# Order of the start of a fused forward and backward kernel: inverse phases earlier, filler transposes out, a small load moved ahead of a large one

## The chip, the cores and the metric

The kernel runs on one core of a Trainium2 chip, as one launch. The metric is device time in microseconds (us), the median of several runs. Engines are named as the profile names them: PE is TensorE's matmul, PEld its weight load, DVE is VectorE, ACT is ScalarE, POOL is GpSimd, SP is SyncE, which issues nearly all DMA transfers here (SPq and ACTq in the profile are the instructions that issue a transfer).

## What is computed

The reference is a forward pass and its whole gradient. With `xn = layernorm(q)`, S = 2048, D = 512, F = 1376, all in bf16, the output is `q + A + B`:

```
ks[t]  = sum over j of k[t-j] * shift_k[:, j]          (4 taps)
kv     = ks * v
y      = irfft(rfft(kv, 2S) * rfft(ssm_k, 2S))[:S] + kv * ssm_D
A      = xn * y
B      = ((xn @ w_gate) * (xn @ w_up)) @ w_down
out    = q + A + B;   then the vjp for grad_out with respect to
         q, k, v, shift_k, ssm_k, ssm_D, w_gate, w_up, w_down
```

So there are ten outputs. The long convolution is done by matrix products with tables of sines (a two stage transform), so the kernel has no FFT.

## The kernel before, in words

The sequence of 2048 rows is laid as 128 partitions times R = 16 rows; the feed-forward part B goes in NCH = 8 chunks of 256 rows, and within a chunk over NFB = 11 blocks of 128 columns of F, two blocks at a time (`ffn1`, L496 to L537). For each pair PE makes `pgu` (gate and up, 16 matmuls, L511) and `pdh` (gradient through w_down, 8 matmuls, L517); ACT copies them out of PSUM as `gu` and `dh` (L235, the helper `act`), and DVE multiplies them into `hd` (L532, L533). `yb` (L539 to L561) makes the products that need a whole chunk, `py` (11 matmuls) and `px` (22).

Beside this main work runs a side generator, `side`: `front()` (L712) and then `groups()` (L737). `front()` normalizes the rows of block b (`norm`, L316: statistics on DVE, a square root on ACT, the scaling of `x_b` on DVE), loads `kh` (all of k, shifted, in three transfers L312 to L314), transposes `ssm_k` (`kernel_spec`, L408: `ptk` on PE, `kn` on ACT) and puts the first transform of three signals through `stage1` (L361): `pf` on PE, copied out as `fst`, by ACT or, for the first signal's even rows, by DVE, and stored. `pre(b)` (L377) makes `dy_b` and `ks_b` (four taps, from `kh`) and `v_b` for that. The mixture of main and side is set by `pace` and `acc` (L770, L875 to L894): after each yield of the main work `acc` grows by `pace`, 170/71, and for each whole 1 the side is driven one step. `acc` starts at `-3 * pace[0]`. The result is a program order; from L657 to the call `first.close()` in `tables` DVE, ACT and PE keep it as written, and afterwards a scheduler may reorder, with `high_priority` (SOON) for evictions.

Transfers: SP issues them in one order, and they use eight semaphores in turn, so a transfer waits until the one eight places before it has landed. The weights come in three pieces, `WPARTS` (L642): blocks 0 and 1, 2 to 5, and 6 to 10. The first is issued from ACT. In the kernel before SP's list starts with x of block 0, grad_out of block 0, the second and third weight pieces with x of block 1 between them, grad_out of block 1, `ssk` (ssm_k, 2 MB, L649), then v 0, x 2, grad_out 2, v 1, and then `skr` (shift_k on one partition, 4 KB, L654) and `Drow` (ssm_D, in the tile `rows`, L655).

Tables: the class `Tables` (L34) makes the phases of the sine tables. The forward ones are made on DVE (`forward_base`, `forward_phases`). For the inverse ones `inverse_base` (L145) takes six small DVE instructions on a column and five on POOL, `inverse_phases` (L159) seven on POOL; its result `tii` is folded on DVE (`inverse_fold`, L174) and goes through the sine on ACT as `zi` (`inverse_sin`, L177). `tables(n)` (L678) places the rest of this behind the steps of chunk 0. `warm(src, n)` (L476) issues n transposes whose result nobody reads; it is called with 36 at the start, 10 after the normalization, and 40 behind the transposes of w_down's third piece (L530).

PSUM: `P2` has three buffers of two banks, used by `pgu`, `pw`, `pf`, `ptk` and `pskb`; `P1` has two of one bank, used by `pdh`, `px`, `py` and the fillers. `pskb` (L709) spreads `skr` over the partitions and becomes `skb`, the tap weights.

Of the kernel before, what the change touches and what calls it, by code (L numbers as in the profile page):

```python
# [8 lines left out]
BF = mybir.dt.bfloat16  # L9
# [9 lines left out]
D = 512  # L19
# [5 lines left out]
NFB = len(FBLK)  # L25
# [165 lines left out]
def kernel(  # L191
# [24 lines left out]
    nc = tc.nc  # L216
# [17 lines left out]
    def act(o, i):  # L234
        nc.scalar.copy(o, i)  # L235
# [16 lines left out]
    def P2(name, shape, dt=F32):  # L252
        return ps2.tile(shape, dt, name=name, tag="p2")

    def P1(name, shape, dt=F32):
        return ps1.tile(shape, dt, name=name, tag="p1")
# [16 lines left out]
    Drow = rows[:, 0, :]  # L273
# [7 lines left out]
    stp = st_es.enter_context(tc.tile_pool(name="stp", bufs=2, side="right"))  # L281
# [4 lines left out]
    WdT = wA.tile([P, NC4, F], BF, name="WdT")  # L286

    hds = [p.tile([P, NFB, 3, 256], BF, name=f"hd{i}") for i, p in enumerate((hdp, hdl))]

    tab_es = ExitStack()  # L290
    TB = Tables(nc, const, wY, tab_es.enter_context(tc.tile_pool(name="tabt", bufs=1, side="right")))
    for t in hds:
        nc.gpsimd.memset(t[96:128, NFB - 1], 0.0)

    XG = {}

# [8 lines left out]
    def load_go(b, x):  # L305
        go = stp.tile([P, 2, D], BF, name="go_b", bufs=3)
        nc.sync.dma_start(go[:], go_n[:, 2 * b:2 * b + 2, :])
        XG[b] = (x, go)
# [11 lines left out]
    def norm_stats(b, root=True):  # L320
        x, go = XG[b]
        stats = stp.tile([P, 2, 6], F32, name="stats", bufs=1)
        rb = slice(2 * b, 2 * b + 2)
        for i in range(2):
            nc.vector.bn_stats(stats[:, i, :], x[:, i, :])
            nc.vector.bn_aggr(mv[:, 2 * b + i, :], stats[:, i, :])
        if root:
            norm_std(b)

    def norm_std(b):  # L330
        rb = slice(2 * b, 2 * b + 2)
        nc.scalar.activation(rstd[:, rb], mv[:, rb, 1], ACTF.Sqrt, bias=eps_t[:, 0:1], scale=1.0)
# [18 lines left out]
    def load_v(b):  # L351
        v = stp.tile([P, 2, D], BF, name="v_b")
        nc.sync.dma_start(v[:], v_n[:, 2 * b:2 * b + 2, :])
        VB[b] = v
# [74 lines left out]
    def wd_transposes(fa, fe):  # L429
        c0, c1 = 128 * fa, min(F, 128 * fe)  # L430
        m = 4 if fe - fa <= 4 else 2
        for ca in range(0, NC4, m):
            pw = P2("pw", [P, m, 16 // m * 128], BF)
            for c in range(ca, ca + m):
                for fb in range(fa, fe):
                    f0, fw = FBLK[fb]
                    nc.tensor.transpose(pw[:, c - ca, (fb - fa) * 128:(fb - fa) * 128 + fw], Wd[:fw, fb, cs(c)], ident[:fw, :fw])
            (act if ca or not fa else dve)(WdT[:, ca:ca + m, c0:c1], pw[:, :, :c1 - c0])
# [26 lines left out]
    def pe_t(src, name, eng):  # L465

        pt = P1("px8", [P, 2 * NC4, P], BF)
        for i in range(2):
            for c in range(NC4):
                nc.tensor.transpose(pt[:, NC4 * i + c, :], src[:, i, cs(c)], ident[:])  # L470
        t = xtp.tile([P, 2, NC4, P], BF, name=name)
        to = t[:].rearrange("p r c s -> p (r c) s")
        eng(to, pt[:])
        return t

    def warm(src, n):  # L476

        pt = P1("warm", [P, P], BF)
        for _ in range(n):
            nc.tensor.transpose(pt[:], src[:], ident[:])  # L480
# [15 lines left out]
    def ffn1(ch):  # L496
        xt, gt = XT.pop(ch)
        hd = hds[ch % 2]
        HD[ch] = hd
        for fb0 in range(0, NFB, 2):  # L500
            blk = FBLK[fb0:fb0 + 2]
            n = len(blk)
            fw = blk[0][1]
            pgu = P2("pgu", [P, 2, 2, 256])
            pdh = P1("pdh", [P, 2, 256])

            def gate_up():
                for i, (f0, w) in enumerate(blk):
                    for t, W in enumerate((Wu, Wg)):
                        for c in range(NC4):  # L510
                            nc.tensor.matmul(pgu[:w, i, t, :], lhsT=W[:, c, f0:f0 + w], rhs=xt[:, :, c, :],  # L511
                                             start=(c == 0), stop=(c == NC4 - 1))

            def down():
                for i, (f0, w) in enumerate(blk):
                    for c in range(NC4):
                        nc.tensor.matmul(pdh[:w, i, :], lhsT=WdT[:, c, f0:f0 + w], rhs=gt[:, :, c, :],  # L517
                                         start=(c == 0), stop=(c == NC4 - 1))

            for f in ((gate_up, down) if ch or fb0 else (down, gate_up)):  # L520
                f()
            if ch == 0 and fb0 == 0:
                wd_transposes(*WPARTS[1])
            gu = gup.tile([P, 2, 2, 256], BF, name="gu")
            dh = gup.tile([P, 2, 256], BF, name="dh")
            act(gu[:fw, :n], pgu[:fw, :n])
            act(dh[:fw, :n], pdh[:fw, :n])
            if ch == 0 and fb0 == 4:
                wd_transposes(*WPARTS[2])
                warm(WdT[:, 0, 0:128], 40)  # L530
            with tc.high_priority(offset=SOON):
                nc.vector.tensor_tensor(hd[:fw, fb0:fb0 + n, 0, :], gu[:fw, :n, 0, :], gu[:fw, :n, 1, :], op=ALU.mult)  # L532
                nc.vector.tensor_tensor(hd[:fw, fb0:fb0 + n, 1:3, :], gu[:fw, :n],  # L533
                                        dh[:fw, :n].unsqueeze(2).to_broadcast((fw, n, 2, 256)), op=ALU.mult)
            if ch < NCH - 1:
                nc.sync.dma_start(HDD[:, fb0:fb0 + n, ch], hd[:, fb0:fb0 + n])
            yield n > 1 and (ch > 4 or fb0 % 4 == 0)  # L537
# [95 lines left out]
    def load_w(eng, fa, fe):  # L633
        c0, c1 = 128 * fa, min(F, 128 * fe)
        full = (c1 - c0) // 128
        eng.dma_start(Wd[:, fa:fa + full, :], B_w_down[c0:c0 + 128 * full, :].rearrange("(fb p) d -> p fb d", p=128))
        if c0 + 128 * full < c1:
            eng.dma_start(Wd[:c1 - c0 - 128 * full, fa + full, :], B_w_down[c0 + 128 * full:c1, :])
        for W, src in ((Wu, B_w_up), (Wg, B_w_gate)):
            eng.dma_start(W[:, :, c0:c1], src[:, c0:c1].rearrange("(c p) f -> p c f", p=128))  # L640
# [5 lines left out]
    x1 = load_q(1)  # L646
    load_w(nc.sync, *WPARTS[2])
    load_go(1, x1)
    nc.sync.dma_start(ssk[:], A_ssm_k.rearrange("(c p) s -> p c s", p=128))  # L649
    load_v(0)  # L650
    load_x(2)
    load_v(1)
    skr = stp.tile([1, D, 4], BF, name="skr", tag="fst", bufs=4)
    nc.sync.dma_start(skr[:], A_shift_k.rearrange("(o d) j -> o d j", o=1))  # L654
    nc.sync.dma_start(Drow, A_ssm_D.rearrange("(o d) -> o d", o=1))  # L655
    first = ExitStack()
    first.enter_context(tc.manual_schedule(engines={nc.vector.engine, nc.scalar.engine, nc.tensor.engine}))  # L657
    warm(ident, 36)
    TB.forward_base()
    norm_stats(0)  # L660
    gt0 = pe_t(XG[0][1], "gt", act)
    wd_transposes(*WPARTS[0])
# [3 lines left out]
    TB.small_phases_w()  # L666
    TB.small_sin_w()
    TB.forward_phases()
    TB.inverse_base()
    TB.inverse_phases()  # L670
    ST = {}

    def open_st1():
# [96 lines left out]
    pace = [170 / 71]  # L770
# [82 lines left out]
    def main():  # L853
        for ch in range(NCH):
            it = ffn1(ch)
            for n, set_here in enumerate(it):
                if ch == 0:
                    tables(n)
                yield set_here
                if n == 1 and 0 < ch < NCH - 1:  # L860
                    load_xt(ch + 1)
                if n == (5 if ch == 1 else 1) and 0 < ch < NCH - 1:
                    while len(WTS) < 2:
                        next(side)
                    yield from yb(ch - 1)
        yield "wa"
        yield from yb(NCH - 2)
        open_c()
        for n, tag in enumerate(yb(NCH - 1)):
            yield tag  # L870
            if 2 < n < 6:
                hid_t(0, n - 3)

    mainit = main()
    acc = -3 * pace[0]  # L875
    mdone = 0
    for tag in mainit:
        if tag == "wa":
# [318 lines left out]
```

## Time and profile before

| what | value |
|---|---|
| runs, us | 487.32, 489.27, 490.5; median 489.27 |
| profiled execution, span from first to last instruction | 486.7 us |
| TensorE clock granted in it | 1.000 |
| PE busy | 473.5 us (97%) |
| DVE, ACT, POOL busy | 339.5 us (70%), 318.0 us (65%), 14.0 us (3%) |
| DMA busy share in tenths, first five slices of 12.2 us | 9 9 9 9 9 |
| moved over the span | 139.87 MB |

The profiled execution has a span of 486.7 us; no time of its own beside the span is listed for it. The span lies 0.6 us below the shortest of the runs and 2.6 us below their median.

In the page the busy share of an engine is an average over the span; a view of waits lists, for an engine, what ended its idle time. A row of the timeline gives start, length, engine, line, operation, output and inputs, count, and in brackets how long the engine had been idle and what ended that.

### The profile page before, as it was taken

Reading aid. Unit: us, or ns where it says so; the run is one execution under the profiler, and the core shown is the slowest. Engines: PE = TensorE matmul, PEld = TensorE weight load, DVE = VectorE, ACT = ScalarE, POOL = GpSimd, SP = SyncE. Lnnn points to the kernel's source line nnn. Section 1 sums busy time; section 2 is a strip of 40 time slices with the busy share of each in tenths; the row PEclk is TensorE's granted clock in tenths of the full one; section 3 lists DMA queues with packets and bytes.
Section 4 is the critical chain, followed back from the end, with each engine's and each line's share of the span. In section 5 each row is a group of like instructions: output and inputs, shape, how many; then the busy total and the mean of one; then the engine's idle time right before and its main releaser. Section 6 shows DMA issues by size and latency. Waiting matters only on the chain.

```text
span 486.7 us, 10581 instructions
## 1 busy us (share of the span) xinstructions
PE 473.5 (97%) x4375; PEld 316.7 (65%) x4375; DVE 339.5 (70%) x623; ACT 318.0 (65%) x354; POOL 14.0 (3%) x30
## 2 busy tenths in 40 slices
PE   8999998899999999999999999999999999999997
PEld 7867753546747638547547743566767787788885
DVE  6699969987366566777857876113256999999860
ACT  4688885758757769779879976275676544344331
POOL 4400000000000000000000000001000000000000
PEclk9999999999999999999999999999999999999999
DMA  9999999998996968968978469999999999599746
GB/s 273 374 375 336 304 239 308 327 337 323 314 303 218 244 193 275 278 196 261 300 227 270 141 216 351 358 324 318 324 378 377 345 366 410 199 285 252 231 152 193
DMA packets 105325, 139.87 MB, mean 287 GB/s; under 512 B 33307, under 2 KB 78784, under 8 KB 103742
## 3 DMA queue, kind: packets, MB, share of 16 engines
q1 hardware_dynamic: 103694, 137.84, 86.3%
q10 hardware_dynamic: 1584, 1.36, 1.0%
q8 instruction: 34, 0.56, 0.5%
q14 instruction: 13, 0.11, 0.1%
HBM read 68.45 MB, written 63.41 MB: 271 GB/s over the span
## 4 chain that ended last, share of the span: by engine, by line
PE 63%; DVE 21%; DMA 10%; issue 2%; ACT 1%; POOL 1%; SPq 1%; ACTq 0%; DVEq 0%
PE pgu L511 12%; PE px L555 12%; PE pu L1032 10%; PE py L548 6%; PE pdh L517 6%; PE pd L996 5%; DMA x_b<-in_A_q_dram 3%; PE ps L584 3%; PE pg L613 3%; PE pt L840 2%; DMA out_dram<-o 2%; DMA hb<-HDD 2%; DVE t_b L392 2%; DVE ks_b L393 1%; DVE fst L238 1%
## 5 line engine op out<-in xcount | busy, mean ns | idle before, releaser
L555 PE MATMUL px<-WT,hd 128*128 128x512 bf16 (+1 forms) x352 | 81.0, 380 | 0.0
L1032 PEld LDWEIGHTS <-xnC 128*128 128x128 bf16 x704 | 67.1, 98 | 8.8 <-issue 0.9
L555 PEld LDWEIGHTS <-hd 128*128 128x128 bf16 (+1 forms) x352 | 32.9, 98 | 44.2 <-issue 7.3
L1032 PE MATMUL pu<-natd,xnC 128*128 128x256 bf16 x512 | 58.5, 273 | 0.2 <-ACT nath L235 0.2
L235 ACT CAST GO<-pg 128x1024 bf16<-128x1024 f32 x48 | 46.2, 1015 | 13.4 <-issue 6.7
L511 PE MATMUL pgu<-xt,Wu 128*128 128x256 bf16 (+1 forms) x352 | 53.1, 273 | 1.5 <-ACT gu L235 1.0
L600 DVE TENSOR_TENSOR T<-SP 128x2048 bf16<-128x2048 bf16 x24 | 29.4, 1223 | 34.8 <-ACT SP L235 34.8
L235 ACT CAST SP<-ps 128x1024 bf16<-128x1024 f32 x48 | 46.5, 1026 | 10.3 <-PE ps L584 8.4
L235 ACT CAST gu<-pgu 128x1024 bf16<-128x1024 f32 (+1 forms) x48 | 45.3, 944 | 11.6 <-PE pgu L511 11.3
L511 PE MATMUL pgu<-xt,Wg 128*128 128x256 bf16 (+1 forms) x352 | 52.8, 273 | 0.0
L517 PE MATMUL pdh<-gt,WdT 128*128 128x256 bf16 (+1 forms) x352 | 47.4, 273 | 0.1
L511 PEld LDWEIGHTS <-Wu 128*128 128x128 bf16 (+1 forms) x352 | 33.1, 100 | 16.2 <-issue 11.7
L548 PE MATMUL py<-Wd,hd 128*128 128x512 bf16 (+1 forms) x176 | 41.2, 380 | 0.0
L235 ACT CAST fst<-pf 128x1024 bf16<-128x1024 f32 x40 | 38.9, 1028 | 1.5 <-issue 1.3
L235 ACT COPY natd<-pt 128x2048 bf16<-128x2048 bf16 x16 | 30.0, 1874 | 14.1 <-PE pt L840 14.1
L235 ACT CAST og<-pu 128x1024 bf16<-128x1024 f32 (+1 forms) x11 | 10.9, 993 | 42.2 <-PE pu L1032 37.7
L517 PEld LDWEIGHTS <-WdT 128*128 128x128 bf16 (+1 forms) x352 | 34.8, 100 | 5.3 <-ACT WdT L235 0.2
L511 PEld LDWEIGHTS <-Wg 128*128 128x128 bf16 (+1 forms) x352 | 34.9, 100 | 3.6
L532 DVE TENSOR_TENSOR hd<-gu 128x512 bf16<-128x512 bf16 (+1 forms) x48 | 19.0, 396 | 21.8 <-ACT gu L235 21.6
L533 DVE TENSOR_TENSOR hd<-gu,dh 128x1024 bf16<-128x1024 bf16 (+1 forms) x48 | 30.8, 642 | 1.0
L996 PE MATMUL pd<-goC,nath 128*128 128x512 bf16 x128 | 30.1, 379 | 0.0
L548 PEld LDWEIGHTS <-hd 128*128 128x128 bf16 (+1 forms) x176 | 16.5, 98 | 20.8 <-issue 3.1
(173 smaller groups left out, 700.8 us busy)
## 6 DMA issues: line engine op xcount, KB each, us to landing
HDD<-hd SPq DMA_DIRECT2D x35, 384.0 KB, 4.0
FD<-fst SPq DMA_DIRECT2D x24, 512.0 KB, 4.8
X<-FD SPq DMA_DIRECT2D x24, 512.0 KB, 4.3
GD<-GO SPq DMA_DIRECT2D x24, 512.0 KB, 3.6
g<-GD SPq DMA_DIRECT2D x12, 1024.0 KB, 8.6
hb<-HDD SPq DMA_DIRECT2D x8, 1344.0 KB, 8.1
bb<-BX SPq DMA_DIRECT2D x8, 512.0 KB, 6.3
BX<-bx SPq DMA_DIRECT2D x7, 512.0 KB, 4.0
```

The lines of the kernel that those rows point to most:

```text
L235: nc.scalar.copy(o, i)
L511: nc.tensor.matmul(pgu[:w, i, t, :], lhsT=W[:, c, f0:f0 + w], rhs=xt[:, :, c, :], start=(c == 0), stop=(c == NC4 - 1))
L517: nc.tensor.matmul(pdh[:w, i, :], lhsT=WdT[:, c, f0:f0 + w], rhs=gt[:, :, c, :], start=(c == 0), stop=(c == NC4 - 1))
L532: nc.vector.tensor_tensor(hd[:fw, fb0:fb0 + n, 0, :], gu[:fw, :n, 0, :], gu[:fw, :n, 1, :], op=ALU.mult)
L533: nc.vector.tensor_tensor(hd[:fw, fb0:fb0 + n, 1:3, :], gu[:fw, :n], dh[:fw, :n].unsqueeze(2).to_broadcast((fw, n, 2, 256)), op=ALU.mult)
L548: nc.tensor.matmul(py[:], lhsT=hd[:fw, fb, 0, ss], rhs=Wd[:fw, fb, :], start=(fb == 0), stop=(fb == NFB - 1))
L555: nc.tensor.matmul(px[:], lhsT=hd[:fw, fb, t, ss], rhs=W[:fw, fb, :], start=(t == 1 and fb == 0), stop=(t == 2 and fb == NFB - 1))
L584: nc.tensor.matmul(ps[32 * q:32 * q + 32, a, :], lhsT=TB.EF[64 * a:64 * a + 64, 4 * g + q, ri].rearrange("p k j -> p (k j)"), rhs=X[64 * a ...
L600: tt(W[:].rearrange("p c a d -> p c (a d)"), A[:, i:i + 1].rearrange("p c a d -> p c (a d)").to_broadcast((P, 2, 2 * D)), B[:].rearrange(" ...
L613: nc.tensor.matmul(pg[q // 2][64 * a:64 * a + 64, q % 2, :], lhsT=TB.EI[32 * q:32 * q + 32, 2 * g + a, yi].rearrange("p k c -> p (k c)"), ...
L996: nc.tensor.matmul(pd[:fw, :], lhsT=nat_h(fb, r), rhs=goC[:, r, :], start=(r == 0), stop=(r == R - 1))
L1032: nc.tensor.matmul(pu[:, c, :, :fw], lhsT=xnC[:, r, cs(c)], rhs=nat_d(fb, r), start=(r == 0), stop=(r == R - 1))
```

## The change

Five edits, of which the last two are not in its name.

1. `inverse_base()` and `inverse_phases()` are called right after `forward_base()`, ahead of the first statistics, and no longer after `forward_phases()`. The order of DVE and POOL changes with that.
2. The 40 fillers behind the transposes of the third piece of w_down are left out.
3. `skr` and `Drow` are loaded ahead of `ssk`, so seven transfers stand at other places in SP's list.
4. The zeroing of the last block's unused partitions of `hd` (two POOL memsets) moves behind the inverse phases in the text; in the built program POOL does one memset, then the first multiplication of the inverse phases, then the other memset.
5. `acc` starts at `-4 * pace[0]`, so the side work starts one yield of the main work later.

```diff
     TB = Tables(nc, const, wY, tab_es.enter_context(tc.tile_pool(name="tabt", bufs=1, side="right")))
-    for t in hds:
-        nc.gpsimd.memset(t[96:128, NFB - 1], 0.0)
...
             if ch == 0 and fb0 == 4:
                 wd_transposes(*WPARTS[2])
-                warm(WdT[:, 0, 0:128], 40)
...
     load_go(1, x1)
+    skr = stp.tile([1, D, 4], BF, name="skr", tag="fst", bufs=4)
+    nc.sync.dma_start(skr[:], A_shift_k.rearrange("(o d) j -> o d j", o=1))
+    nc.sync.dma_start(Drow, A_ssm_D.rearrange("(o d) -> o d", o=1))
     nc.sync.dma_start(ssk[:], A_ssm_k.rearrange("(c p) s -> p c s", p=128))
     load_v(0)
     load_x(2)
     load_v(1)
-    skr = stp.tile([1, D, 4], BF, name="skr", tag="fst", bufs=4)
-    nc.sync.dma_start(skr[:], A_shift_k.rearrange("(o d) j -> o d j", o=1))
-    nc.sync.dma_start(Drow, A_ssm_D.rearrange("(o d) -> o d", o=1))
...
     TB.forward_base()
+    TB.inverse_base()
+    TB.inverse_phases()
+    for t in hds:
+        nc.gpsimd.memset(t[96:128, NFB - 1], 0.0)
     norm_stats(0)
...
     TB.forward_phases()
-    TB.inverse_base()
-    TB.inverse_phases()
     ST = {}
...
-    acc = -3 * pace[0]
+    acc = -4 * pace[0]
```

In the built program the order of PE, DVE, ACT and SP differs through `front()`; from about the place that PE reaches at 133.6 us in the profile before, the first `ps` of `groups()`, the instructions stand in the same order in both. Of SP's list, with the old places: the transfer of `hd`'s blocks 8 and 9 now stands ahead of `kh`'s first part, and the store of the normalized rows of block 2 (XN, L349) stands ahead of `kh`'s second and third part, where it stood ahead of the third alone. On PE, `dy` of block 1 stands behind the 11 matmuls of the second `py`, and `dy` of block 4 behind 22 matmuls of `px`, which came after it before.

## The prediction

> **What bounds the kernel.** I read the granted clock first, then PE's waits, the timeline of the first 32 us, the chain, and busy time by stretches.
>
> ```profile
> core 0: 486.7 us, clock 1.000
> ```
> ```profile
> PE 473.5 (97%) x4375; PEld 316.7 (65%) x4375; DVE 339.5 (70%) x623; ACT 318.0 (65%) x354; POOL 14.0 (3%) x30
> ...
> PE 63%; DVE 21%; DMA 10%; issue 2%; ACT 1%; POOL 1%; SPq 1%; ACTq 0%; DVEq 0%
> ```
>
> PE is busy for 473.5 of 486.7 us at full clock, so only its 13.2 us of idleness and the fillers (work for nobody) can be won. Yet a third of the chain is DVE and DMA: early on the two lie level with PE. PE's waits name the places:
>
> ```profile
> PE pf L369 <- DVE dy_b L382: 1.8, 1, 1.8
> PE warm L480 <- POOL ident masks.py:199: 1.4, 1, 1.4
> PE pf L369 <- ACT fst L235: 1.3, 1, 1.3
> PE pgu L511 <- ACT gu L235: 1.0, 1, 1.0
> PE pskb L709 <- DMA skr<-in_A_shift_k_dram: 1.0, 1, 1.0
> ```
>
> The fourth and fifth are what the change goes for. The timeline shows the fourth:
>
> ```profile
> 15.03 3.64 POOL L172 TENSOR_SCALAR tii<-pb 128x256 int32<-128x256 f32 x4
> ...
> 18.32 2.40 PE L480 MATMUL warm<-ident,WdT 128*128 128x128 bf16 x40
> 18.71 0.69 DVE L73 TENSOR_SCALAR tii<-tii 128x1024 int32<-128x1024 int32 x1 [3.08 <-POOL tii L172]
> 19.22 0.24 SPq L655 DMA_DIRECT2D rows<-in_A_ssm_D_dram  x1
> ...
> 19.43 1.06 ACT L76 ACTIVATE zi<-tii 128x1024 bf16<-128x1024 int32 x1 [3.99 <-DVE tii L73]
> ...
> 20.70 0.99 ACT L235 CAST gu<-pgu 128x1024 bf16<-128x1024 f32 x1
> ...
> 21.75 0.60 PE L511 MATMUL pgu<-xt,Wu 128*128 128x256 bf16 x4 [1.03 <-ACT gu L235]
> ```
>
> POOL ends the phases at 18.67; DVE waits 3.08 us for them, ACT 3.99, and PE cannot start the next pgu before the gu copy has freed its buffer (21.69). The 40 fillers lie inside that wait: without the first edit, leaving them out wins nothing. Next, the load of k:
>
> ```profile
> 30.34 0.34 SPq L312 DMA_DIRECT2D kh<-in_A_k_dram  x1
> 30.74 0.45 SPq L313 DMA_DIRECT2D kh<-in_A_k_dram  x1
> 36.40 0.34 SPq L349 DMA_DIRECT2D XN<-x_b  x1
> 36.79 0.44 SPq L314 DMA_DIRECT2D kh<-in_A_k_dram  x1
> ```
> ```profile
> 42.09 0.69 DVE L390 TENSOR_TENSOR ks_b<-kh,skb 128x1024 bf16<-128x1024 bf16 x1 [0.35 <-DMA kh<-in_A_k_dram]
> ```
> ```profile
> 0.00:30.00 30.00, 25.88 (x291) 22.84 (x292) 20.88 (x65) 18.96 (x23) 11.22 (x28) 1.00 0.99 334
> 30.00:60.00 30.00, 29.57 (x256) 22.74 (x254) 29.32 (x55) 25.19 (x29) 0.00 (x0) 1.00 0.96 332
> ```
>
> The columns are stretch, its length, busy time of PE, PEld, DVE, ACT and POOL, clock, DMA share, GB/s. DMA is full (0.99, then 0.96), DVE is busy 29.3 of 30 us, and DVE needed kh just when it had landed. The last part of kh stood behind the store XN of block 2, which waited 5.1 us for DVE's scaling of x (SP's waits), and landed 5.2 us after its issue (kh's own view), at 42.0.
>
> **The change part by part.** The sum is made against the profiled span, 486.7 us, which lies 2.6 below the median of the runs, 489.27 (0.6 below the shortest); I take the difference off the median.
>
> *Phases earlier.* POOL's patterns end at 3.17. Then come two memsets (1.41 together), pa 0.62, five columns (about 1.1), pb 0.94 and 1.19, tii 3.64: 8.9 us, to about 12.1 in place of 18.67. DVE's six columns (0.9 us) go where DVE waited for x (3.24 to 4.42), at no cost; were x earlier they would cost up to 0.9. Nothing else is queued on POOL. DVE's fold then follows tiv's fold (ends 15.62): 15.6 to 16.3, the sine starts at 16.35 instead of 19.43. So ACT is 3.08 us ahead, gu is freed at 18.6 and PE may start pgu at 18.67 instead of 21.75.
>
> *Fillers out.* PE's last transpose ends at 18.5, so the 2.40 us go with the wait. What is late next: the third weight piece. SP issued `rows` at 19.22 after waiting for Wg, so Wg landed at about 19.2; the half of pgu that reads it could start at 19.1: 0.15 us lost. Further on px of x waits for the dh copy (ACT, 23.2 against PE's 22.8): 0.4. Bounds: no loss, or a wait to 19.9 as for the transfer behind, 0.7.
>
> *shift_k ahead.* skr's wait, 0.97 us, goes. skr and rows have 5 KB; ssk is issued two places later (13.9 instead of 11.25), but the queue holds a backlog until it lands at 25.5 (its issue to landing is 14.3 us), so it lands as before, and ptk wants it at 26.3.
>
> *PE's lead.* From pgu to the first pf PE has 10.0 us of work in the new order (pgu 40 and pdh 25 matmuls at 0.109; ptk 1.09, px 0.49 twice, pskb 0.87), so pf starts at 18.67 + 0.55 + 10.0 = 29.2 instead of 31.71, with 1.4 us more work done (chunk 0's last blocks): a lead of 3.9 us.
>
> *The later side (acc) and SP's order.* Here the lead meets kh. The DMA queue is full to 46 us, and a transfer lands when what stands before it has been moved. In the new list hd of blocks 8 and 9 (384 KB, at 382 GB/s 1.0 us) stands ahead of kh, everything else ahead is the same. So kh lands at about 42.0 + 0.95 = 42.9 (bounds: 42.0 if order does not matter, 45 if the parts behind XN are issued late). DVE's work up to the first ks_b is the same set; it is 3.1 us ahead, less 0.3 for two copies, so it stands waiting from 38.9 to 42.9, with ks_b, the two hd products and the eviction fst of row 6 behind: 0.7 + 0.9 + 1.13. By the waits in the built program the pf of row 7 needs that eviction's buffer: 45.7. PE arrives there after 12.9 us of work by the same rows and 0.4 of small waits, at 42.5, so **it waits 3.2 us**. Before, PE had done that much work by 46.66: the lead left is 0.9.
>
> *60 to 100 us.* DVE was at ks_b at 42.09 and is now at 43.0, but dy of block 1 no longer stands behind the statistics of block 4's late x, and hd blocks SP less, so x of blocks 4 and 5 is issued 1 to 2 us earlier. PE's old 1.3 us wait for fst is replaced by one of 1.5 to 2.1: in ACT's new order the square root of block 5 stands ahead of dy 1's copy. The lead at 84 us is 0.3 to 0.9; I take 0.6. The 1.81 us wait for dy 4:
>
> ```profile
> 96.64 0.66 DVE L382 TENSOR_TENSOR dy_b<-go_b,x_b 128x1024 bf16<-128x1024 bf16 x1
> ```
> ```profile
> 97.35 0.60 PE L369 MATMUL pf<-dy_b,W 128*128 128x512 bf16 x2 [1.81 <-DVE dy_b L382]
> ```
>
> Now 22 px (4.75 us) stand ahead of it: PE comes 4.75 - 0.6 = 4.1 us later than its 95.5, and dy 4 is ready by 97.3 or sooner. The wait goes. From 100 to 290 us PE idles 0.14 us, and the order is the same from 133.6: the lead is carried to the end.
>
> Sum: 3.9 - 3.0 (kh) - 0.3 + 1.8 = **2.4 us**, span 484.3, median 489.27 - 2.4 = 486.9.
>
> A rule to weigh is the clock. The first 36 transposes, after idleness, took 4.02 us, the 40 later ones 2.40 (2.16 for 36): coming from idle cost 1.9 us; no wait up to 1.8 us in mid-kernel lowered the clock. The Trainium skill (TensorE: Matmul & The Clock Gate, Part 1: The HAM clock gate) says that PE falls to half clock after about 3.4 us idle and needs as long to return. That page's figures would price one such fall at an estimated 1.7 us. No trace here shows a wait of that length in mid-kernel.
>
> **The rivals.**
>
> *B: the lead is kept.* kh lands early enough, or PE finds other buffers. Then 3.9 + 1.8 = 5.7 us are won: 483.6. For it: the kh wait was only 0.35. Against: it was that short because DMA and DVE were level, and one of them now comes earlier alone.
>
> *C: nothing is won.* The wait at pf of row 7 lasts long enough to cost a slow start as at 0 us: 1.9 more, and the dy 4 wait goes anyway. 2.4 - 1.9 leaves 0.5: 488.8. For it: the wait forecast, 3.2 us, is far longer than any in the trace of before. Against: it may be shorter by pieces. (By the skill's rule 3.2 us is just short of the limit.)
>
> *D: slower.* Two parts of kh now stand behind XN of block 2, which needs x of that block scaled on DVE, forecast at 33.6. If that came after the queue has run dry (41), kh would land 5.2 us after its issue, as its last part did. Each us costs PE one. It decides from kh at 45.3; with x scaled at 41 kh lands at 47.4: 2.1 us slower than before, 491.4. Against: before, with DVE 3 us later, that scaling ended at 36.3.
>
> **How the numbers follow.** The forecast of 486.9 gets 0.5 (own range 485.5 to 488.3: kh's bounds 42.0 and 44, and 0.3 on the mid part), B 0.2, C 0.2, D 0.1. The runs of before differ by 3.2 us, so 1% (4.9 us: under 484.4 or over 494.2) is about what a measurement of this kernel can tell from no change. Half of B, and a little of the rest, lies under 484.4: faster 0.12. D passes 494.2 only with kh later than 50.2: slower 0.04. Same 0.84. For 8 in 10 the range takes in most of B and C and the low part of D: 483.5 to 490.2.
>
> **What would show it.** tii's last POOL row ends near 12.1; zi starts near 16.4; pgu follows the transposes within 1 us at full clock; pskb has no wait. DVE's ks_b waits about 4 us for kh and PE's pf about 3 us for fst; if neither is there, B holds. Matmuls of 128x512 longer than 0.38 us each near 46 us would speak for C. kh later than 45 would be D. dy 4 should have no wait; if it has, the 1.8 us are wrong. I am wrong in the whole if a wait that was not there appears after 133.6 us.

## The result and the profile after

The changed kernel takes 487.07 us, the median of 13 runs (484.65 to 488.81); the kernel before, beside it, 488.77 us (13 runs, 487.23 to 491.27). The ratio is 0.9941, 95% interval 0.9915 to 0.9967: by it 2.9 us faster (1.6 to 4.2); the two medians alone differ by 1.7 us. The profiled execution has a span of 486.3 us and took 488.18 us, 1.1 above the median; the spans of the other runs reach from 482.7 to 486.9.

The cores' line, then the page's busy times and chain:

```profile
core 0: 486.3 us, clock 0.999
```
```profile
PE 468.3 (96%) x4293; PEld 314.7 (65%) x4335; DVE 340.6 (70%) x623; ACT 318.2 (65%) x354; POOL 14.0 (3%) x30
PE 59%; DMA 17%; DVE 16%; SPq 3%; issue 2%; ACT 1%; ACTq 0%
```

PE has 4293 matmuls against 4335 weight loads, so 42 matmul records are missing and PE's busy time reads low. The count before was 4375; the difference of 40 loads is the fillers. PE's waits (engine, line, what ended them, us in total, times, longest):

```profile
PE pf L367 <- DVE fst L238: 2.4, 2, 2.0
PE pf L367 <- ACT fst L235: 2.1, 1, 2.1
...
PE pt L839 <- DVE kd L1059: 1.2, 1, 1.2
PE po L970 <- DMA g<-GD: 1.0, 1, 1.0
```

The waits for gu and for skr at the front are gone, and the one for dy_b too. At the head of the list stand two others. The front in the timeline:

```profile
8.69 4.09 POOL L172 TENSOR_SCALAR tii<-pb 128x256 int32<-128x256 f32 x4
...
15.70 0.69 DVE L73 TENSOR_SCALAR tii<-tii 128x1024 int32<-128x1024 int32 x1
...
16.42 1.06 ACT L76 ACTIVATE zi<-tii 128x1024 bf16<-128x1024 int32 x1 [0.46 <-DVE tii L73]
...
18.83 0.60 PE L509 MATMUL pgu<-xt,Wu 128*128 128x256 bf16 x4
...
19.72 0.61 PE L509 MATMUL pgu<-xt,Wg 128*128 128x256 bf16 x4 [0.29 <-DMA Wg<-in_B_w_gate_dram]
```

POOL is done at 12.78 in place of 18.67, the sine starts 3.0 us earlier, and PE goes on to pgu at once. The load of k, on SP's queue and then on DVE and PE:

```profile
29.36 0.35 SPq L310 DMA_DIRECT2D kh<-in_A_k_dram  x1
33.98 0.34 SPq L347 DMA_DIRECT2D XN<-x_b  x1
34.38 0.42 SPq L311 DMA_DIRECT2D kh<-in_A_k_dram  x1
34.85 0.43 SPq L312 DMA_DIRECT2D kh<-in_A_k_dram  x1
```
```profile
39.15 0.24 DVE L324 BATCH_NORM_AGGREGATE mv<-stats 128x2 f32<-128x6 f32 x2
...
42.68 0.69 DVE L388 TENSOR_TENSOR ks_b<-kh,skb 128x1024 bf16<-128x1024 bf16 x1 [3.29 <-DMA kh<-in_A_k_dram]
...
44.23 1.22 DVE L238 CAST fst<-pf 128x1024 bf16<-128x1024 f32 x1
...
45.50 1.02 PE L367 MATMUL pf<-kn,W 128*128 128x512 bf16 x3 [1.99 <-DVE fst L238]
```

DVE comes to ks_b 2.35 us earlier than before (39.39 against 41.74), and kh lands 0.6 later, so DVE stands for 3.29 us with the eviction fst behind it, and PE stands for that eviction. By stretches (busy time of PE, PEld, DVE, ACT, POOL; clock, DMA share, GB/s) the queue is as full as before:

```profile
0.00:30.00 30.00, 27.55 (x280) 23.80 (x280) 24.01 (x73) 21.43 (x26) 11.21 (x28) 1.00 0.99 337
30.00:60.00 30.00, 26.88 (x234) 20.52 (x238) 26.27 (x46) 22.92 (x28) 0.00 (x0) 1.00 0.95 335
```

And dy of block 4, which PE used to wait for, is now ready long before PE comes:

```profile
94.78 0.66 DVE L380 TENSOR_TENSOR dy_b<-go_b,x_b 128x1024 bf16<-128x1024 bf16 x1
95.01 4.92 PE L552 MATMUL px<-WT,hd 128*128 128x512 bf16 x22
99.77 1.03 PE L367 MATMUL pf<-dy_b,W 128*128 128x512 bf16 x4
```

PE's lead over the profile before, place by place: 1.95 at the first pf (with 1.4 us more work done), 1.2 at the pf of row 7 (45.50 against 46.66, the time by which PE had done as much work before), 2.33 near 100 us, 2.56 at the first ps (131.08 against 133.64), 2.47 until 381 us, and 0.45 at PE's last matmul, mostly since the waits for kd (1.21 against 0.60) and g (0.96 against none) in the last quarter came out longer.

### The profile page after: what moved, and what is told of

Read it like the earlier page. It is cut to its first block, busy times and chain, and to the rows that moved or that the text cites. A ratio compares the mean times of both kernels' runs of the same rounds, so it can differ in the third digit from the quotient of the medians.

```text
span 486.3 us, 10468 instructions
## 1 busy us (share of the span) xinstructions
PE 468.3 (96%) x4293; PEld 314.7 (65%) x4335; DVE 340.6 (70%) x623; ACT 318.2 (65%) x354; POOL 14.0 (3%) x30
## 4 chain that ended last, share of the span: by engine, by line
PE 59%; DMA 17%; DVE 16%; SPq 3%; issue 2%; ACT 1%; ACTq 0%
PE pgu L509 13%; PE px L552 13%; PE pdh L515 6%; PE py L545 6%; PE pu L1031 6%; DMA hb<-HDD 4%; DMA Wg<-in_B_w_gate_dram 4%; DMA out_dram<-o 3%; PE ps L581 3%; PE pg L610 3%; PE pt L839 2%; PE pd L995 2%; PE pf L367 2%; DMA kh<-in_A_k_dram 2%; DVE dk L1086 2%
## 5 line engine op out<-in xcount | busy, mean ns | idle before, releaser
L552 PE MATMUL px<-WT,hd 128*128 128x512 bf16 (+1 forms) x339 | 78.6, 380 | 1.6 <-issue 1.4
L545 PE MATMUL py<-Wd,hd 128*128 128x512 bf16 (+1 forms) x168 | 40.1, 380 | 0.7 <-issue 0.5
L597 DVE TENSOR_TENSOR U<-SP 128x2048 bf16<-128x2048 bf16 x24 | 29.2, 1217 | 0.0
```

The lines of the kernel that those rows point to most:

```text
L545: nc.tensor.matmul(py[:], lhsT=hd[:fw, fb, 0, ss], rhs=Wd[:fw, fb, :], start=(fb == 0), stop=(fb == NFB - 1))
L552: nc.tensor.matmul(px[:], lhsT=hd[:fw, fb, t, ss], rhs=W[:fw, fb, :], start=(t == 1 and fb == 0), stop=(t == 2 and fb == NFB - 1))
L597: tt(W[:].rearrange("p c a d -> p c (a d)"), A[:, i:i + 1].rearrange("p c a d -> p c (a d)").to_broadcast((P, 2, 2 * D)), B[:].rearrange(" ...
```

## The experiments

All are timed against the kernel before. The table has the ratio with its interval, and from one profile each the first pf, PE's wait at the pf of row 7 near 45 us, and the first ps. Where acc is -4, about 1.4 us more work stands ahead of the first pf. The runs were made on three chips (e1, e2, e3 and a_kh_split; e5 to e8; e9 to e12), each beside runs of the kernel before on that chip.

| run | edits against | ratio (95%) | first pf | wait | first ps |
|---|---|---|---|---|---|
| before | | 1 | 31.71 | 0 | 133.64 |
| changed | | 0.9941 (0.9915 to 0.9967) | 29.76 | 1.99 | 131.08 |
| e9, changed again | | 0.9951 (0.9918 to 0.9984) | 29.76 | 1.59 | 128.62 |
| e1, fillers out | before | 1.0061 (1.0037 to 1.0085) | 33.56 | 0 | 134.67 |
| e2, phases early | before | 0.9998 (0.9974 to 1.0023) | 31.79 | 0 | 132.89 |
| e3, both | before | 1.0105 (1.0072 to 1.0138) | 36.91 | 0 | 137.23 |
| e10, acc -4 | before | 0.9980 (0.9952 to 1.0009) | 34.52 | 0 | 131.49 |
| e5, phases late | changed | 0.9945 (0.9915 to 0.9976) | 34.14 | 0 | 131.89 |
| e6, shift_k behind | changed | 0.9890 (0.9852 to 0.9928) | 30.35 | 1.17 | 130.35 |
| e7, acc -3 | changed | 0.9984 (0.9960 to 1.0008) | 33.27 | 0 | 134.53 |
| e12, phases late, 12 fillers | changed | 1.0023 (0.9994 to 1.0051) | 34.06 | 0 | 132.68 |
| a_kh_split, k split at row 4 | changed | 1.0043 (1.0014 to 1.0073) | 29.76 | 0 (3.72 near 40) | 133.06 |
| e8, k split at row 8 | changed | 0.9894 (0.9855 to 0.9932) | 29.82 | 0.38 | 128.36 |
| e11, e8 and shift_k behind | changed | 0.9912 (0.9879 to 0.9946) | 30.15 | 0.23 | 128.84 |

The theory: the front's lead is real, the load of k takes most of it back, and what stays comes from the order of the side work. The rivals: the front is the gain; kh is not what takes it.

**e1, fillers out alone.**

```diff
                 wd_transposes(*WPARTS[2])
-                warm(WdT[:, 0, 0:128], 40)
```

> The kernel before with one edit, the 40 empty transposes left out. My theory: the phases still end at 18.67 on POOL, so PE stands 3.3 to 3.4 us (18.4 to 21.75) ahead of pgu in place of 1.03, the first pf stays at 31.7, the first ps at 133.6, and the time is that of before (ratio 1.000, within 0.003). Rival 'fillers are the cost': pgu starts up to 2.4 us earlier and the ratio is 0.995. Rival 'slow clock after a long wait' (C of the prediction): the 128x256 matmuls behind the wait take longer than their 0.109 us each, the first pf comes 1 to 2 us later than 31.7 and the ratio is 1.002 to 1.004.

PE did wait for the phases, 2.96 us, at full clock behind it in this execution, and gained nothing there, as forecast. But the kernel became slower, and the front shows another wait:

```profile
21.81 0.60 PE L511 MATMUL pgu<-xt,Wu 128*128 128x256 bf16 x4 [2.96 <-ACT gu L235]
...
30.73 1.01 ACT L235 CAST gu<-pgu 128x1024 bf16<-128x1024 f32 x1 [2.58 <-PE pgu L511]
31.64 1.87 ACT L235 COPY kn<-ptk 128x2048 bf16<-128x2048 bf16 x1
...
33.56 0.38 PE L369 MATMUL pf<-kn,W 128*128 128x512 bf16 x1 [1.83 <-ACT kn L235]
```

On ACT a gu copy now stands ahead of the first kn copy. The scheduler changed that order when the fillers left; the theory had missed it. At the first ps 1.0 us of the loss is there; the rest of the 0.6% comes later. In ten of its eleven executions the mean granted clock is 0.997 or less, so the wait may lower the clock in others; the one profile does not show it.

**e2, phases early alone.**

```diff
-    for t in hds:
-        nc.gpsimd.memset(t[96:128, NFB - 1], 0.0)
...
     TB.forward_base()
+    TB.inverse_base()
+    TB.inverse_phases()
+    for t in hds:
+        nc.gpsimd.memset(t[96:128, NFB - 1], 0.0)
     norm_stats(0)
...
     TB.forward_phases()
-    TB.inverse_base()
-    TB.inverse_phases()
```

> The kernel before with one edit, the inverse phases made early (the 40 empty transposes stay, shift_k stays behind). My theory: tii ends near 12.8 as in the changed kernel, but PE is busy with the empty transposes until 20.7, so pgu starts near 20.8, 1.0 earlier; then PE waits for skr until the same 25.9, 2.0 us in place of 0.97, and the first pf stays at 31.7 to 31.9: no gain, ratio 1.000. Rival 'the phases alone are the gain': the first pf comes 1 us earlier or more, ratio 0.998 or below.

As the theory had it: pgu at 21.07, a wait of 1.77 us for skr until 26.07, the first pf at 31.79, ratio 0.9998.

**e3, both.** The edits of e1 and e2.

> The kernel before with two edits, phases early and the empty transposes out; shift_k still behind ssm_k, acc as before. My theory: pgu starts at 18.8, the lead of 3 us is lost at once at pskb, where PE waits for skr until 25.9, 3.5 to 4 us; first pf at 31.7 or a little above, ratio 1.000. Rival 'shift_k was only in the way by chance': skr lands as early as PE comes, pf starts at 28.7 and the ratio is 0.994. Rival 'slow clock': matmuls after the wait of 3.5 to 4 us are longer, pf later than 32.5, ratio 1.003.

The wait for skr was 3.90 us, as forecast, and the slow clock, the rival, came with it. PE's rows behind the wait, then the clock by stretches (its column is the third from the end):

```profile
26.28 1.65 PE L708 MATMUL pskb<-skr,rows 1*128 1x512 bf16 x4 [3.90 <-DMA skr<-in_A_shift_k_dram]
...
31.68 1.06 PE L509 MATMUL pgu<-xt,Wg 128*128 128x256 bf16 x4
...
33.38 0.60 PE L509 MATMUL pgu<-xt,Wg 128*128 128x256 bf16 x4
```
```profile
26.30:28.30 2.00, 2.00 (x9) 0.76 (x10) 0.00 (x0) 1.01 (x1) 0.00 (x0) 0.56 1.06 395
28.30:30.30 2.00, 2.00 (x22) 2.00 (x21) 1.37 (x3) 0.00 (x0) 0.00 (x0) 0.50 1.01 363
...
32.30:34.30 2.00, 2.00 (x16) 1.56 (x14) 0.30 (x1) 0.22 (x1) 0.00 (x0) 0.73 1.08 319
```

Four matmuls take 1.06 us instead of 0.60, from about 26.6 to 33.4. Half of those 6.8 us, 3.4, is lost, and the 1.83 us for kn come on top: together about the 5.2 us by which the first pf is late. e1, which has the same wait for kn and no slow stretch, has its first pf 3.35 us earlier. Two of the change's edits together cost 1% without the others.

**a_kh_split, k's load split at row 4.**

```diff
-        nc.sync.dma_start(ST["kh"][:, 3:3 + R, :], k_n)
+        nc.sync.dma_start(ST["kh"][:, 3:3 + 4, :], k_n[:, 0:4, :])
         nc.sync.dma_start(ST["kh"][1:113, 0:3, :], k_n[0:112, R - 3:R, :])
         nc.sync.dma_start(ST["kh"][113:128, 0:3, :], k_n[112:127, R - 3:R, :])
+        nc.sync.dma_start(ST["kh"][:, 3 + 4:3 + R, :], k_n[:, 4:R, :])
```

> The changed kernel with one further edit: k's load is split, its first 4 rows of 16 (512 KB) and the two small shifted parts go first, the other 12 rows behind them, so block 0's taps need 1.5 MB less of the full queue. My theory (kh takes back the lead won at the front): the part that block 0 needs lands near 38.5 to 40, ks_b waits under 1 us in place of 3.29, PE's 1.99 us wait for fst near 45 goes, the first ps comes at 129 to 130 in place of 131.1, and the time falls by 1 to 2 us, ratio to before 0.990. Rival 'DVE is the bound there': ks_b comes early but fst does not, the wait is only moved and the first ps stays at 131, ratio 0.994. Rival 'the queue': later loads (rest of k, x of blocks 3 to 5) come late and the wait near 77 grows by what was won.

With 1.5 MB less ahead of it kh landed 3.9 us earlier (ks_b at 38.75 against 42.68), as the queue's rate has it. But the time grew. In the built program ks_b now stands ahead of two fst evictions on DVE:

```profile
38.75 0.69 DVE L389 TENSOR_TENSOR ks_b<-kh,skb 128x1024 bf16<-128x1024 bf16 x1 [4.19 <-DMA kh<-in_A_k_dram]
...
39.96 1.22 DVE L238 CAST fst<-pf 128x1024 bf16<-128x1024 f32 x1
...
41.23 0.60 PE L510 MATMUL pgu<-xt,Wu 128*128 128x256 bf16 x4 [3.72 <-DVE fst L238]
...
42.10 0.68 PE L510 MATMUL pgu<-xt,Wu 128*128 128x256 bf16 x4
42.57 1.06 PE L510 MATMUL pgu<-xt,Wg 128*128 128x256 bf16 x4
```

PE stood 3.72 us and ran at half clock from 42.5 to 45.9. So the run says where kh lands, and nothing on what the time would be with kh early.

**e8, split at row 8.** The same edit with 8 in place of 4; fst stays ahead of ks_b.

> The changed kernel with k's load split at row 8 of 16 (first half and the two small parts ahead of the second half). In the split at row 4 the first part landed at 38.7 and the scheduler had put ks_b so far ahead on DVE that it waited all the same; with 8 rows the fst copies stand ahead of ks_b as in the changed kernel. My theory: the first part lands near 40.0, ks_b waits about 1 us in place of 3.29, PE's wait for fst near 45 falls from 1.99 to under 0.5, first ps at 129.2 to 130, ratio 0.990. Rival 'given back later': the wait near 77 grows by as much, first ps at 131, ratio 0.994.

```profile
40.54 0.69 DVE L389 TENSOR_TENSOR ks_b<-kh,skb 128x1024 bf16<-128x1024 bf16 x1 [1.24 <-DMA kh<-in_A_k_dram]
...
42.68 1.22 DVE L238 CAST fst<-pf 128x1024 bf16<-128x1024 f32 x1
...
43.96 1.02 PE L368 MATMUL pf<-kn,W 128*128 128x512 bf16 x4 [0.38 <-DVE fst L238]
```

The wait at row 7 fell to 0.38, so PE is 1.5 us ahead of the changed kernel there. Of that 1.0 is given back at 51 us, at a new wait for a later fst (DVE has little slack in this stretch), and 0.4 comes back at 57, where the changed kernel waits for another. The first ps came at 128.36, earlier than forecast, and the ratio is 0.9894: close to what rival B of the prediction had (5.7 us), and better than the changed kernel's, though the two intervals overlap. How much of the 2.7 us at the first ps is the split's own is put in question by e9.

**e5, phases late.** The changed kernel with the two calls put back behind `forward_phases()`.

> The changed kernel with the inverse phases put back behind the forward ones; all else as changed, with the same order on DVE and ACT from 20 us on. My theory (kh takes back most of the front's lead): POOL ends the phases near 18.7, PE waits about 3.0 us at pgu, the first pf comes near 32.4 in place of 29.76, kh lands at the same 42.7, so PE's 1.99 us wait for fst near 45 is gone, and at the first ps only 0.6 to 1.0 us of the 2.6 are still missing: 131.7 to 132.1 in place of 131.1, ratio to before 0.995 to 0.996. Rival 'the front's lead is the gain': nothing is given back, first ps at 133.7, ratio 0.999 or 1.000. Rival 'slow clock' already at 3.0 us: matmuls behind the wait at 0.21 us each, first ps past 134.

This is the sharpest test. The front loses 4.4 us (first pf 34.14 against 29.76): 3.26 us of waiting, and about 1.7 by half clock behind it, which the theory had not expected at 3.0, less 0.6 that the changed kernel loses for Wg and at the start:

```profile
22.05 0.60 PE L509 MATMUL pgu<-xt,Wu 128*128 128x256 bf16 x4 [3.26 <-ACT gu L235]
...
23.08 1.06 PE L509 MATMUL pgu<-xt,Wu 128*128 128x256 bf16 x4
23.93 1.06 PE L509 MATMUL pgu<-xt,Wg 128*128 128x256 bf16 x4
```

kh had landed when DVE came to ks_b at 43.68, so nothing waited for it. At the pf of row 7 (47.72, no wait) 2.2 of the 4.4 are left, and at the first ps 0.8. Against the changed kernel's second profile (e9) they are 2.6 and 3.3. So the profiles show kh taking back about half of the front's lead, and leave open what becomes of the other half. The ratio is that of the changed kernel: the first edit that the title names is worth nothing that these runs can tell, though the intervals leave room for some 2 us.

**e6, shift_k behind.** `skr` and `Drow` back to their old place.

> The changed kernel with shift_k and ssm_D loaded behind, as before; all else as changed. My theory: with acc at -4 PE comes to pskb only near 25.4, skr lands at 25.9 to 26.3, so the wait is 0.4 to 0.8; it is swallowed at kh: first ps at 131.1 to 131.3, ratio 0.994. Rival 'shift_k ahead is worth its 0.97 us': first ps at 132, ratio 0.996.

A wait of 0.54 us at pskb, and 0.8 us less of waiting at row 7 (1.17 against 1.99). The first ps came 0.75 us earlier than forecast, and the ratio, if anything, lies below the changed kernel's. Moving shift_k brings nothing that shows once acc is -4.

**e7, acc at -3.**

```diff
-    acc = -4 * pace[0]
+    acc = -3 * pace[0]
```

> The changed kernel with acc at -3 again; all else as changed. The scheduler then puts a gu copy ahead of the first kn copy on ACT, as in the two kernels without empty transposes that have been run. My theory: PE waits 1.8 us for kn at the first pf as there; hd of blocks 8 and 9 goes behind kh again, so kh lands about 0.9 earlier, near 41.8; dy 4's wait of 1.6 to 1.8 us near 96 is back; first ps at 132.5 to 133.5, ratio 0.997 to 1.000. Rival 'acc does nothing': first ps at 131, ratio 0.994. Rival 'hd ahead of kh is the larger loss': first ps below 130.5, ratio under 0.992.

The gain is gone: 1.83 us for kn, as forecast, 1.54 for dy 4, and 1.47 for ssm_k at ptk, which had not been foreseen: without the later side work PE comes to ptk before ssk has landed. Behind that wait PE ran at half clock from 26.1 to 29.5, which costs 1.7 us in this profile:

```profile
25.57 1.62 PE L412 MATMUL ptk<-ident,ssk 128*128 128x128 bf16 x16 [1.47 <-DMA ssk<-in_A_ssm_k_dram]
...
27.41 1.06 PE L509 MATMUL pgu<-xt,Wu 128*128 128x256 bf16 x4
```

The gain is gone without that fall too: in 7 of the 12 executions the mean granted clock is 0.998 or more, and they take 489.8 us in the mean, against 488.0 for the two such executions of the kernel before on that chip. Nothing waited for kh (ks_b started at 43.25), so the run does not say when it landed.

**e9, the changed kernel again.**

> The changed kernel once more, beside the three below on one chip. My theory: the first ps at 130.9 to 131.4 again; the late waits (po for g, pt for kd), which took 1.6 us of the lead in its first profile, differ from execution to execution, so the end's lead over the kernel before lies anywhere from 0.4 to 2.5; ratio 0.994. Rival 'the late loss belongs to the change': the same two waits of 1.0 and 1.2 us again.

The first ps was forecast at 130.9 to 131.4 and came at 128.62; the late losses differed too (0.63 for kd, none for g, but 1.51 for khC). Of the 2.5 us, 0.4 stand at row 7 (45.11 against 45.50) and 2.1 are the wait near 77. In the first profile:

```profile
69.49 0.69 DVE L388 TENSOR_TENSOR ks_b<-kh,skb 128x1024 bf16<-128x1024 bf16 x1 [1.96 <-DMA KS<-ks_b]
...
75.66 1.28 DVE L323 BATCH_NORM_STATS2 stats<-x_b 128x6 f32<-128x512 bf16 x2 [0.92 <-DMA x_b<-in_A_q_dram]
...
77.73 0.29 ACT L330 ACTIVATE rstd<-mv,eps_t 128x2 f32<-128x2 f32 x1 [2.37 <-DVE mv L324]
...
78.97 0.59 PE L367 MATMUL pf<-v_b,W 128*128 128x512 bf16 x2 [2.13 <-ACT fst L235]
```

and in the second, in the same order of instructions:

```profile
67.58 0.69 DVE L388 TENSOR_TENSOR ks_b<-kh,skb 128x1024 bf16<-128x1024 bf16 x1 [0.45 <-DMA KS<-ks_b]
...
73.08 1.29 DVE L323 BATCH_NORM_STATS2 stats<-x_b 128x6 f32<-128x512 bf16 x2 [0.25 <-DMA x_b<-in_A_q_dram]
...
75.15 0.29 ACT L330 ACTIVATE rstd<-mv,eps_t 128x2 f32<-128x2 f32 x1 [1.00 <-DVE mv L324]
```

DVE waits until the last store of a ks_b buffer has landed, 1.96 us in one execution and 0.45 in the other; x of block 5 is issued behind it, and the square root on ACT stands ahead of the fst that PE needs. A first ps from one profile is thus good to some 2 us, no better; the ratios have to carry the verdicts.

**e10, acc -4 alone.** The kernel before with that one edit.

> The kernel before with one edit, acc at -4. My theory (most of the front's lead is swallowed at kh, and the shift of the side work wins the net): pskb comes past 27, so PE no longer waits for skr; the first pf at 32 to 32.5 with 1.4 us more work done; no wait above 0.5 us near 45; dy 4's wait of 1.8 us is gone; first ps at 131.0 to 132.0, close to the changed kernel's 131.1, ratio 0.995. Rival 'the front's edits are the gain': only dy 4's wait is won or not even that, first ps at 132 to 133.6, ratio 0.997 to 1.000.

The first ps is as forecast, the rest is not. The first pf came at 34.52, 2 us later than forecast, behind waits of about 1.0 each for gu, dh and kn. The ratio is 0.998, not told apart from 1: two waits of 1.0 us for X behind the first ps and one of 1.0 for khC, absent in the first profile of the changed kernel, took the lead back. At a mean granted clock of 0.998 or more this kernel takes 488.6 us (11 executions), and so does the kernel before on that chip (9 executions). The theory falls in its plain form: acc alone does not win the net.

**e11, split and shift_k behind.**

> The split at row 8 and shift_k with ssm_D behind as before; all else as changed, with the same order on PE, DVE and ACT as the split alone. My theory: a wait of about 0.5 us at pskb, the rest as in the split; first ps at 128.4 to 129.0, ratio 0.989 to 0.990: shift_k ahead brings at most 0.5 us. Rival 'shift_k ahead costs': as in the changed kernel with shift_k behind, whose ratio of 0.989 lay below the changed kernel's 0.994, the time falls further, first ps below 128.2, ratio 0.986.

The first ps is as forecast, the wait at pskb is 0.3, and the ratio of 0.9912 lies just above the range. Beside e9 on the same chip the medians are 485.27 and 487.77, but the intervals of the two ratios overlap: faster than before for certain, and faster than the changed kernel by all signs, not beyond doubt.

**e12, phases late with 12 fillers.** e5 with `warm(WdT[:, 0, 0:128], 12)` behind the transposes.

> The changed kernel with the inverse phases late, and 12 of the 40 empty transposes (0.7 us) kept ahead of the wait. My theory: PE's wait at pgu is 3.26 less 0.7, 2.5 us, as the run with 2.96 us below the limit, so the matmuls behind it keep 0.109 us each, and the first pf comes near 32.5 in place of 34.1; kh swallows it, first ps at 131 to 132. Rival 'the slow stretch did not come from the wait': 0.21 us each again, first pf near 34.

The wait was 1.70 us and no slow matmul came behind it. That does not show a limit, since in e7 a wait of 1.47 us was followed by half clock. The first pf was late all the same: PE was 1.2 us behind e5 before the wait, after a longer slow stretch at the start, and waited 1.11 for a dh copy. The scheduler's order is another one, and the ratio is 0.8% above that of e5, so acc at -4 does not carry the gain with these fillers in. It says nothing further.

## Why the prediction was right

The time was forecast at 486.9 and is 487.07; the ratio says 2.9 us where the sum said 2.4. The main terms are there in the traces, the front's lead, what kh takes of it and the wait for dy 4. That the time agrees to 0.2 us is luck: the sum was taken off a median of three runs, 0.5 us above that of the thirteen, its steps missed by up to 1.2 us in both directions, and the two profiles of the changed kernel end 0.45 and 3.4 us ahead of the profile before. (The prediction's own range takes 44 as kh's late bound where its working has 45; by 45 it would reach 489.3. The result lies inside either.) The steps, with the first and the second profile of the changed kernel:

| step | forecast | measured |
|---|---|---|
| POOL done | 12.1 | 12.78 |
| sine zi | 16.35 | 16.42 |
| pgu | 18.67 | 18.83 |
| lost for Wg (start of the second pgu group against 0.44 behind the first) | 0.15 | 0.45 and 0.29 |
| first pf | 29.2 | 29.76 and 29.76 |
| ks_b starts | 42.9 | 42.68 and 42.29 |
| DVE stands for kh | 4.0 | 3.29 and 2.90 |
| PE stands at row 7 | 3.2 | 1.99 and 1.59 |
| lead left there | 0.9 | 1.2 and 1.55 |
| wait at v 1 | 1.5 to 2.1 | 2.13 and 0 |
| wait for dy 4 | gone | gone |
| lead near 100 us | 2.4 | 2.33 and 4.79 |

*The front and kh.* Right in mechanism, and nearly in size: DVE stands for kh in both profiles, and in e8, where kh lands earlier, PE's wait at row 7 shrinks to 0.38. The wait at row 7 was 1.2 us too long in the forecast, mainly because PE came there at 43.5 and not 42.5; 0.6 us of that are there at the first pf, half of them from the longer wait for Wg.

*A cost that the sum set at nothing.* PE was 0.5 us later than before from 8 us on (pdh at 9.00, not 8.49). The six columns on DVE were done by 3.98, before x came, so they were free as forecast. But DVE's scaling of x_b, for which PE waits there, took longer:

```profile
6.68 0.74 DVE L341 TENSOR_SCALAR x_b<-x_b,mv,rstd 128x512 bf16<-128x512 bf16 x2
```
```profile
6.87 1.06 DVE L339 TENSOR_SCALAR x_b<-x_b,mv,rstd 128x512 bf16<-128x512 bf16 x2
```

The first row is before, the second changed. In all nine profiles with the phases early this row takes 0.81 to 1.11 us and ends at 7.93 to 7.97 whenever it starts, and pdh starts at 9.00 to 9.04, also where the transposes ahead of it ran at full speed (e9). In the five with the phases late the row takes 0.73 or 0.74, and pdh starts at 8.49 to 8.84, but for e12 with its slow start. So making the phases early costs PE 0.2 to 0.5 us there. POOL works on pb in that time (6.84 to 7.78); that this is what holds DVE up is likely, not shown.

*Order of the middle part.* The gain of 1.8 us at dy 4 is there, and e7, which undoes acc, has that wait back. The wait at v 1 was taken for sure and is a matter of the execution.

*Carried to the end.* This step failed: the lead of 2.47 shrank to 0.45 in the first profile and, in the second, from 5.2 to 3.4. The prediction had counted waits only to 290 us, and had named a new wait behind 133.6 as a sign that the whole is wrong; one came (0.96 for g), yet the whole holds, since such waits come and go with the execution (e9 has none for g, and 1.51 for khC).

*Rival C* has a true mechanism, and it was not far: half clock followed waits of 3.26, 3.72 and 3.90 us, and also of 1.47 and 2.02 us. In the two profiles of the changed kernel the waits of 1.99 and 1.59 us at row 7 were not followed by it. *Rival B* is not what the change does (the wait for kh is there in both profiles), though the split comes near its time. *D* did not come up: XN of block 2 was issued at 33.98.

*The clock of each execution.* The sum has no term for it. The runs list the mean granted clock of each execution. On the chip of e9 to e12 the kernel before had 0.998 or more in about a third of its executions (9, mean 488.6 us), and the others took 2.5 us longer; the changed kernel had it in 6 of 12 (mean 486.8 us). So at like clock the gain is 1.8 us there, where the ratio of e9 says 2.4. The profile before, from which the sum was made, has a clock of 1.000, so where the other executions lose theirs is not shown.

What the prediction lacked is what e1, e3 and e7 show: that leaving out the fillers alone changes ACT's order and costs 0.6%, and that acc at -4 mends it. The phases alone and the fillers alone bring nothing (e2, e1), and the changed kernel loses nothing that shows without the early phases (e5) or without shift_k ahead (e6). Six versions have acc at -4 and none of the 40 fillers. All but a_kh_split, whose ks_b was moved, lie at 0.989 to 0.995 (changed, e5, e6, e8, e11), and no other version lies below 0.998. They share one order of ACT's early copies and of the later side work, with kn ahead of gu and dy 4 behind px. That this order is the gain fits these five, but it was argued and not tested alone: no run has only acc at -4 and the fillers out. Why e10, with the same acc, lacks the gain is seen in one profile alone (the waits for X). That stays open.

## What to carry to other kernels

A lead won ahead of a saturated queue is worth only what the queue's next delivery lets through: ask first when that lands, and put the part that is needed first at its head (e8 does so; its gain over the changed kernel is likely, not certain). Where a scheduler orders the engines, a dummy instruction left out or a load split can reorder copies far away, so read the new order on every engine before pricing an edit. A single profile places a late wait only to within what the transfers vary; run it twice before a mechanism is read from it, and compare executions of like granted clock.

## What the runs showed of the hardware

The clock of PE. Five profiles have a stretch of half clock in mid-kernel, in which the clock column reads 0.50 and 128x256 matmuls take 0.21 us each in place of 0.109. Three stand behind waits of 3.26 (e5), 3.72 (a_kh_split) and 3.90 us (e3), but two behind shorter ones, of 1.47 us (e7) and of 2.02 us (e6, far behind the front):

```profile
464.33 1.07 PE L970 MATMUL po<-IW,g 128*128 128x128 bf16 x16 [2.02 <-DMA g<-GD]
465.23 2.94 PE L1031 MATMUL pu<-natT,xnC 128*128 128x256 bf16 x14
```

The slow stretch began 0.3 to 1.3 us behind the end of the wait and lasted 3.4 us, in e3 6.8. Waits of 1.70 (e12), 1.99 (changed) and 2.96 us (e1) were followed by none. So the length of a wait alone does not decide it, and these runs do not show what else does. The Trainium skill (TensorE: Matmul & The Clock Gate, Part 1: The HAM clock gate) gives about 3.4 us of idleness, and as much of work to return, counted in a free-running window; the length of the slow stretches here agrees with that, the idleness does not, since 1.47 us was enough in e7.

The start. The 36 transposes at the start took 4.02 us in ten of the fourteen profiles and 3.55 to 3.84 in the others. How long the slow stretch lasted behind them differed, with the same instructions: the first 8 real ones took 0.62 us before, 1.03 in the first profile of the changed kernel and 0.62 in its second, and in e12 the three groups of 8 that follow the start took 1.03, 1.06 and 1.06. In e12 PE was 1.2 us later behind them than in e5; in the two profiles of the changed kernel it came to the next pdh at 9.00 all the same. The profile's clock column read 1.00 over these first 10 us in all of them, while it read 0.50 in the slow stretches later.
